# One transfer queue, straight casts and 168 transfers: a rewritten order for a clustered attention with a gated convolution behind it

## The chip, the cores and the metric

The kernel runs on one core of a Trainium2 chip. The metric is the device time of one execution in microseconds (us), lower is better; it is the span from the first to the last instruction plus about 2 us around it. PE is TensorE, DVE is VectorE, ACT is ScalarE, POOL is GpSimd, and SP is the sync engine, which here does nothing but issue DMA transfers.

## The reference

Four batches of eight heads, 768 tokens, 64 dimensions a head. Each token attends only to the tokens of its own cluster, where a cluster is the nearest of 16 centroids of that head. The attention's output (512 columns for a token) runs through a gated FFN with a convolution of three taps along the tokens.

```python
q_assign = argmax(einsum('bhsd,hcd->bhsc', q_n, c_n))   # and k_assign; q_n, k_n, c_n normalized
mask = q_assign[:, :, :, None] == k_assign[:, :, None, :]
scores = where(mask, q @ k^T / sqrt(64), -1e9)
x = softmax(scores) @ v                                  # heads side by side: (4, 768, 512)
h = maximum(x @ w_in, 0)                                 # 512 -> 1024
conv = sum of conv_w[k] * (h shifted by k - 1 along the tokens)
out = (h * sigmoid(conv)) @ w_out                        # 1024 -> 512
```

Inputs and outputs are float32 in HBM; q, k and v are 6.3 MB each.

## The kernel before, in words

The work goes by pairs of heads: `g` = 0 to 15, four pairs to a batch. Pair `g` is loaded, brought into a layout with the 64 dimensions on the partitions, assigned to clusters, and then used by two units `t`, one for each half of the queries: `t = 8 * batch + 4 * half + pair`, 0 to 31.

There is no loop that orders the work. A string `PLAN` lists some 1,660 steps, and each engine executes its own steps in the order of the string. SP is one such engine: a transfer waits there for its data and for its buffer, and all later ones on SP wait behind it. Steps that matter here, with the line of the profile:

- `LQ.g.part`, `LK.g.part` (L248, L255) load q and k on SP; `lq`, `lk` do the same from ScalarE's queue. `LV`/`lv` (L262, L264) load v. The string `KIND` gives each pair a way to be transposed. A pair of kind T is loaded by head (two parts, 128 partitions of 64-element rows) and transposed by PE: `T.g.c` (L275, four transposes into one PSUM bank), `Qd`/`Qa` copy it to `qkT`. A pair of kind B is loaded in four parts of 32 partitions (rows of 32 elements) and transposed in 32 x 32 blocks by VectorE: `D.g.o` (L283).
- `A.g` (L303) multiplies `qkT` with the centroids, `M0.g` to `M6.g` (L327 to L366) find the argmax on VectorE and write a code of the cluster into `pack`, `K.g` (L371) transposes `pack` on PE, `Bd`/`Ba` copy it to `spk`, and `BX.g` (L381, L383; `BA` from ScalarE's queue) transfers it into three rows of `ext`, the bias rows, which make the mask part of the score matmul.
- The 64 rows of `ext` above them are q and k in float16, for each head at partitions 0 to 63. `CQp.g.o` casts a whole `qkT` (128 partitions, both heads) into `c`, and `CX.g.h` (L294) transfers 64 partitions of `c` into `ext`. A few casts go straight: `CDa.g.h.o` casts head `h`'s 64 partitions of `qkT` into `ext`. The letter behind (p, a, d) names the engine: POOL, ScalarE, VectorE.
- `S.t.i` (L398) makes the scores, two matmuls for 256 keys; `E.t.i` (L410) takes the exponential on ScalarE; `V.t.u` (L429) multiplies with v and a column of ones; `NR`, `N` (L440, L445) normalize on VectorE into `x`.
- `XD.t` (L467) turns `x` by a DMA transpose into `xT`; `X.t` (L460) does it by three PE transposes, with `Ya`/`Yd` copying the result.
- `I` (L483) is x @ w_in, `Ra`/`Rd` (L496, L498) the relu into `hpad`, `c`, `a`, `b` and `cw`, `aw`, `bw` (L515, L517) the convolution, `H`/`Hw` the tanh, `G`/`Gw` (L554) the gate, `O` (L566) the product with w_out, `Fa`/`Fd` (L579, L581) its evacuation, `FX.b.tq` (L584) the store of 128 tokens.
- `_wl`/`_wlq` load a piece of the weights on SP or ScalarE's queue, `_wp`/`_wd` cast it, `_tp` builds matrices of taps on POOL, `_k` issues filler matmuls early on.

`qkT`, `c` and the v staging have two buffers each, `qk_in` four, `ext` and `v16` five.

Of the kernel before, what the change touches and what calls it, by code (L numbers as in the profile page):

```python
# [8 lines left out]
F32 = mybir.dt.float32  # L9
# [5 lines left out]
KIND = "TTTTTTTBBBBBBBBB"  # L15
# [129 lines left out]
def kernel(  # L145
# [11 lines left out]
    nc = tc.nc  # L157
# [425 lines left out]
    def store(b, tq):  # L583
        nc.sync.dma_start(out[b, P * tq : P * (tq + 1), :], o_t.pop((b, tq))[:])  # L584
# [246 lines left out]
```

## Time and profile before

| | |
|---|---|
| median of 3 runs | 268.18 us (267.23 to 268.81) |
| the profiled execution | 267.05 us, its span 265.1 us |
| mean granted clock of PE | 0.966 |
| busy: PE, DVE, ACT, POOL | 235.7, 212.5, 209.2, 63.6 us |
| transfers issued | 226: 190 by SP, 36 by ScalarE |
| DMA bytes | 38.75 MB |
| DMA queue of SP / of ScalarE | 30.68 MB, 56.9% / 7.69 MB, 16.2% of the span of 16 engines |

Busy times are unions of an engine's instructions. Matmuls are pipelined and short gaps between them count as busy, so PE's 89% is an upper figure. The granted clock tells in slices how fast PE was allowed to run. The chain that ended last is a path back through the execution: at each step what released an instruction.

### The profile page before, as it was taken

Reading aid. Unit: us, or ns where it says so; the run is one execution under the profiler, and the core shown is the slowest. Engines: PE = TensorE matmul, PEld = TensorE weight load, DVE = VectorE, ACT = ScalarE, POOL = GpSimd, SP = SyncE. Lnnn points to the kernel's source line nnn. Section 1 sums busy time; section 2 is a strip of 40 time slices with the busy share of each in tenths; the row PEclk is TensorE's granted clock in tenths of the full one; section 3 lists DMA queues with packets and bytes.
Section 4 is the critical chain, followed back from the end, with each engine's and each line's share of the span. In section 5 each row is a group of like instructions: output and inputs, shape, how many; then the busy total and the mean of one; then the engine's idle time right before and its main releaser. Section 6 shows DMA issues by size and latency. Waiting matters only on the chain.

```text
span 265.1 us, 6230 instructions
## 1 busy us (share of the span) xinstructions
PE 235.7 (89%) x2385; PEld 146.0 (55%) x2385; DVE 212.5 (80%) x414; ACT 209.2 (79%) x325; POOL 63.6 (24%) x107
## 2 busy tenths in 40 slices
PE   7878699979699985899989989996979999999994
PEld 7565376657365642566445545663345666565541
DVE  5777735875649996999999789995783999999971
ACT  5636758979498997699989889997567999995841
POOL 7313400463334353430450334000320000000000
PEclk9999979999799999799999999999797999999999
DMA  8986979999989697598979982775693220011244
GB/s 164 244 195 189 234 184 212 315 209 161 154 220 191 90 191 87 108 146 144 158 184 164 185 165 55 181 110 90 127 251 117 67 72 2 1 38 45 79 150 167
DMA packets 114825, 38.75 MB, mean 146 GB/s; under 512 B 106473, under 2 KB 108265, under 8 KB 114796
## 3 DMA queue, kind: packets, MB, share of 16 engines
q1 hardware_dynamic: 89470, 30.68, 56.9%
q10 hardware_dynamic: 25326, 7.69, 16.2%
q8 instruction: 18, 0.29, 0.5%
q14 instruction: 11, 0.09, 0.1%
HBM read 23.11 MB, written 6.29 MB: 111 GB/s over the span
## 4 chain that ended last, share of the span: by engine, by line
PE 40%; DMA 25%; DVE 18%; ACT 6%; issue 4%; SPq 4%; ACTq 1%; POOL 0%; DVEq 0%; POOLq 0%
PE sc L398 12%; PE flex L566 8%; DMA ext<-spk 7%; PE flex L483 6%; DVE cnv L517 6%; PE flex L429 6%; DMA qk_in<-in_q_dram 6%; DMA qk_in<-in_k_dram 5%; DMA ext<-c 4%; ACT attn L410 4%; DVE qkT L283 3%; SPq L248 3%; DMA xT<-x 2%; DVE hg L554 2%; PE flex L275 2%
## 5 line engine op out<-in xcount | busy, mean ns | idle before, releaser
L410 ACT ACTIVATE attn<-sc 128x768 f16<-128x768 f32 x192 | 146.7, 818 | 23.2 <-PE sc L398 22.3
L398 PE MATMUL sc<-ext 128*128 128x384 f16 x384 | 93.7, 336 | 13.5 <-DMA ext<-spk 6.7
L517 DVE SCALAR_TENSOR_TENSOR cnv<-hpad,cwcol,cnv 128x768 f16<-128x768 f16 (+2 forms) x72 | 63.8, 903 | 0.2
L429 PEld LDWEIGHTS <-attn 128*128 128x128 f16 x1152 | 51.4, 100 | 16.1 <-issue 3.2
L398 PEld LDWEIGHTS <-ext 128*128 128x128 f16 x384 | 33.5, 100 | 43.8 <-issue 20.6
L429 PE MATMUL flex<-v,attn 128*128 128x65 f16 x1152 | 54.9, 196 | 1.0 <-DVE x L445 1.0
L566 PE MATMUL flex<-w_out,hg 128*128 128x512 f16 x176 | 48.7, 390 | 0.0
L235 POOL CAST c<-qkT 128x768 f16<-128x768 f32 x26 | 25.2, 980 | 95.6 <-DVE qkT L283 28.3
L483 PE MATMUL flex<-xT,w_in 128*128 128x384 f16 x228 | 46.0, 329 | 1.8 <-DMA xT<-x 1.5
L483 PEld LDWEIGHTS <-w_in 128*128 128x128 f16 x256 | 23.9, 98 | 17.9 <-issue 3.4
L554 DVE SCALAR_TENSOR_TENSOR hg<-th,hpad 128x768 f16<-128x768 f32 (+3 forms) x34 | 31.4, 935 | 0.0
L545 ACT ACTIVATE th<-cnv 128x768 f32<-128x768 f16 (+2 forms) x30 | 25.6, 852 | 5.4 <-DVE cnv L517 5.3
L566 PEld LDWEIGHTS <-hg 128*128 128x128 f16 x192 | 18.1, 99 | 15.6 <-issue 0.9
L496 ACT ACTIVATE hpad<-flex 128x384 f16<-128x384 f32 x45 | 22.1, 517 | 1.4 <-PE flex L483 1.2
L283 DVE STREAM_TRANSPOSE qkT<-qk_in 128x768 f32<-128x768 f32 x18 | 17.2, 965 | 6.8 <-DMA qk_in<-in_q_dram 6.8
L303 PE MATMUL flex<-qkT,cT 128*32 128x384 f32 x128 | 13.8, 503 | 4.6 <-DVE x L445 4.1
L445 DVE TENSOR_TENSOR x<-flex,rec 128x384 f16<-128x384 f32 x32 | 17.5, 546 | 0.3
L235 POOL CAST v<-v_in 128x768 f16<-128x768 f32 x13 | 12.3, 957 | 16.0 <-DMA v_in<-in_v_dram 15.9
L327 DVE STREAM_TRANSPOSE sim<-flex 128x384 f32<-128x384 f32 x16 | 9.2, 576 | 7.0 <-PE flex L303 7.0
L515 DVE TENSOR_SCALAR cnv<-hpad,cwcol 128x768 f16<-128x768 f16 (+2 forms) x36 | 13.7, 382 | 0.7 <-ACT hpad L496 0.5
L440 DVE RECIPROCAL rec<-flex 128x6 f32<-128x6 f32 x32 | 5.9, 183 | 10.0 <-PE flex L429 9.9
L579 ACT ACTIVATE o_sb<-flex 128x512 f32<-128x512 f32 x17 | 10.0, 602 | 4.8 <-PE flex L566 4.8
(81 smaller groups left out, 193.2 us busy)
## 6 DMA issues: line engine op xcount, KB each, us to landing
out_dram<-o_sb SPq DMA_DIRECT2D x24, 256.0 KB, 3.2
ext<-c SPq DMA_DIRECT2D x30, 192.0 KB, 4.8
v_in<-in_v_dram SPq DMA_DIRECT2D x10, 384.0 KB
qk_in<-in_k_dram SPq DMA_DIRECT2D x28, 96.0 KB, 3.3
qk_in<-in_q_dram SPq DMA_DIRECT2D x27, 96.0 KB, 3.8
qk_in<-in_q_dram SPq DMA_DIRECT2D x12, 192.0 KB, 4.5
v_in<-in_v_dram ACTq DMA_DIRECT2D x6, 384.0 KB
qk_in<-in_k_dram SPq DMA_DIRECT2D x11, 192.0 KB, 4.6
```

What stands on the lines that cost most here:

```text
L235: (nc.vector if name == "d" else nc.gpsimd).tensor_copy(out=to, in_=src)
L283: nc.vector.transpose(qkT_of(g)[:, o, :], qk_t[g][:, o, :])
L398: nc.tensor.matmul(s[:, n, 0:HS], lhsT=ext_b[g % NE][:, h, 1, P * (kt + n) : P * (kt + n + 1)], rhs=ext_b[g % NE][:, h, 0, HS * a : HS * ( ...
L410: nc.scalar.activation(attn[t, i // 3][:, kt : kt + 2, :], sc[(6 * t + i) % 2][:, :, 0:HS], AF.Exp, scale=0.125)
L429: nc.tensor.matmul(avp(at)[:, u, 0 : D + 1], lhsT=attn[t, h][:, kt, P * jq : P * (jq + 1)], rhs=v16_b[g % NE][:, h, kt, 0 : D + 1], start= ...
L445: nc.vector.tensor_tensor(out=x16[t].rearrange("p jq (h d) -> p h jq d", h=2), in0=av[:, :, 0:D].rearrange("p (h jq) d -> p h jq d", h=2), ...
L483: nc.tensor.matmul(bank[at][:, 0:HS], lhsT=w_in16[:, r, 2 * u + f, :], rhs=xT[:, b % 2, r, HS * a : HS * (a + 1)], start=(r == 0), stop=(r ...
L496: nc.scalar.activation(to, src, AF.Relu)
L517: nc.vector.scalar_tensor_tensor(out=cnv, in0=src, scalar=w, in1=cnv, op0=ALU.mult, op1=ALU.add)
L545: nc.scalar.activation(th, cnv_t[key].rearrange("p (f s) -> p f s", s=N), AF.Tanh, scale=0.5)
L554: nc.vector.scalar_tensor_tensor(out=hg_b[b][:, 2 * u + fs.start : 2 * u + fs.stop, lo : lo + N], in0=th, scalar=1.0, in1=hpad(b, u)[:, fs ...
L566: nc.tensor.matmul(bank[at][:, 0:Dm], lhsT=hg_b[b][:, fb, P * tq : P * (tq + 1)], rhs=w_out16[:, fb, :], start=(fb == 0), stop=(fb == NFB ...
```

## The change

1. `KIND` has eight pairs of kind T (0 to 7) instead of seven; pairs 8 to 15 are of kind B.
2. k of a pair of kind T can be loaded whole by one transfer, both heads with 128 partitions outermost (`LK.g` without a part). Pairs 1 to 7 use it; pair 0's k comes in two parts from ScalarE's queue.
3. All casts of q and k go straight into `ext`, four for a pair over 64 partitions each: 51 on POOL (`CDp`), 7 on VectorE (`CDd`), 6 on ScalarE (`CDa`). No `CX` transfers and no `c` tile are left.
4. Batches 0 to 2 store two blocks of 128 tokens by one transfer (`FX.b.i`, i = 0 to 2), out of an `o_sb` of two blocks; batch 3 stores each block by itself.
5. The eight units of batch 0 turn `x` on PE (`X` with 4 `Ya` and 4 `Yd`) instead of by DMA; 20 `XD` remain, and 12 units use PE in all, for 28 and 4.
6. ScalarE's queue carries three transfers (the centroids and pair 0's k); everything else is on SP: 165.
7. The order of the whole `PLAN` is new, with small shifts of steps between engines (relus on VectorE 17 for 12, copies of `qkT` 15 and 9 for 13 and 8, output evacuations on VectorE 4 for 6).

Steps of each kind in the two orders:

| step | before | after | | step | before | after |
|---|---|---|---|---|---|---|
| LQ + lq | 50 | 48 | | CQ (p, a, d) | 30 | 0 |
| LK + lk | 50 | 41 | | CD (p, a, d) | 4 | 64 |
| LV + lv | 16 | 16 | | T | 21 | 24 |
| CX | 30 | 0 | | D | 18 | 16 |
| BX + BA | 18 | 18 | | X | 4 | 12 |
| XD | 28 | 20 | | Rd / Ra | 12 / 52 | 17 / 47 |
| FX | 24 | 15 | | Fd / Fa | 6 / 18 | 4 / 20 |
| _wl + _wlq | 8 | 8 | | V, S, E, I, O, K, A | the same | the same |

The diff, with the order cut to the stretches that the text speaks of:

```diff
-KIND = "TTTTTTTBBBBBBBBB"
+KIND = "TTTTTTTTBBBBBBBB"
...
+    "_par _k.32@4 T.0.0@0 _pk.0 _hz.2 lk.0.1 lk.0.0 _n0 _n1 _zd.0.0 _nq _n2 _n5 Qd.0.0 _k.16@4 T.0.1@1 Qd.0.1 "
+    "T.0.2@2 Qa.0.2 _pk.2 _hpk.0 _zp.0.1 _zp.1.1 CDp.0.0.0 LQ.1.0 LQ.1.1 LK.1 _n3@0 T.1.0@1 _n4 _k.2@4 A.0@2 "
...
+    "M6.0.0 _k.5@4 K.0.1@1 CDa.0.1.1 Ba.0.1 _k.12@4 T.2.0@1 T.2.2@2 T.2.1@0 Qa.2.2 BX.0.1 LK.3 K.0.0@3 Ba.0.0 "
+    "M3.1.0 M1.1.1 BX.0.0 LQ.3.0 LQ.3.1 M2.1.1 M4.1.0 M3.1.1 M5.1.0 M6.1.0 M4.1.1 _v.0 CVd.0 M5.1.1 Qa.2.0 "
...
-    "Qa.3.2 CQp.2.0 _zp.2.1 CVp.0 CQp.2.1 BX.1.0 T.3.0@1 LV.2 CX.2.1 CX.2.0 _cw0 S.1.0 E.1.0 LV.3 V.0.0@3 K.2@2 "
-    "S.1.1 V.0.1@3 V.0.2@3 S.1.2 Qd.3.0 Bd.2 Qd.3.1 CQp.3.1 _wp.2 _pk.0 A.3@0 M0.3 M1.3 M2.3 M3.3 M4.3 M5.3 "
+    "M6.2 Qd.3.0 K.2@0 Bd.2 Qd.3.1 S.0.5 V.0.0@1 V.0.1@1 S.1.0 A.3@2 BX.1.1 LV.2 _cw0 _wl.1 BX.2 LK.4 LQ.4.1 "
+    "LQ.4.0 LV.3 _wl.0 E.0.5 E.1.0 S.1.1 V.0.2@1 S.1.2 V.0.3@1 _cw1@0 E.1.1 S.1.3 E.1.2 S.1.4 V.0.4@1 M0.3 M1.3 "
...
+    "Gw.1.3.1 aw.1.3.0 BX.12 LK.14.1 LK.14.0 LV.14 LQ.14.0 LK.14.3 LQ.14.1 Ba.13 LQ.14.2 Ra.19.1 E.23.0 E.23.1 "
+    "LQ.14.3 BX.13 LQ.15.2 LK.14.2 LK.15.2 LK.15.1 LK.15.3 LQ.15.0 LK.15.0 LQ.15.3 LQ.15.1 S.23.2 E.23.2 "
...
+        elif part is None:
+            queue.dma_start(to[:, o, :], src[b, h0 : h0 + 2].rearrange("h (p j) d -> p j h d", p=P))
...
     def evac(name, b, tq):
-        o_t[b, tq] = rot.tile([P, Dm], F32, name="o_sb", tag="o_sb", bufs=BUFS["o_sb"])
-        src = bank[out_at[b, tq]][:, 0:Dm]
+        n = 1 if b == B - 1 else 2
+        if (b, tq // n) not in o_t:
+            o_t[b, tq // n] = rot.tile([P, 2, Dm], F32, name="o_sb", tag="o_sb", bufs=BUFS["o_sb"])
+        src, to = bank[out_at[b, tq]][:, 0:Dm], o_t[b, tq // n][:, tq % n, :]
...
+    def store(b, i):
+        if b == B - 1:
+            nc.sync.dma_start(out[b, P * i : P * (i + 1), :], o_t.pop((b, i))[:, 0])
+        else:
+            to = out[b, 2 * P * i : 2 * P * (i + 1), :].rearrange("(x p) d -> p x d", x=2)
+            nc.sync.dma_start(to, o_t.pop((b, i))[:])
```

More of the change, by code (lines that the diff above doesn't have):

```diff
@@ L575, in evac @@
     def evac(name, b, tq):
-        o_t[b, tq] = rot.tile([P, Dm], F32, name="o_sb", tag="o_sb", bufs=BUFS["o_sb"])
-        src = bank[out_at[b, tq]][:, 0:Dm]
+        n = 1 if b == B - 1 else 2
+        if (b, tq // n) not in o_t:
+            o_t[b, tq // n] = rot.tile([P, 2, Dm], F32, name="o_sb", tag="o_sb", bufs=BUFS["o_sb"])
+        src, to = bank[out_at[b, tq]][:, 0:Dm], o_t[b, tq // n][:, tq % n, :]
         if name == "a":
-            nc.scalar.activation(o_t[b, tq][:], src, AF.Copy, scale=0.5)
+            nc.scalar.activation(to, src, AF.Copy, scale=0.5)
         else:
-            nc.vector.tensor_scalar(out=o_t[b, tq][:], in0=src, scalar1=0.5, scalar2=None, op0=ALU.mult)
-    def store(b, tq):
-        nc.sync.dma_start(out[b, P * tq : P * (tq + 1), :], o_t.pop((b, tq))[:])
+            nc.vector.tensor_scalar(out=to, in0=src, scalar1=0.5, scalar2=None, op0=ALU.mult)
+    def store(b, i):
[4 more added lines that the diff above has]
+            nc.sync.dma_start(to, o_t.pop((b, i))[:])
     w_t = {}
```

227 rows, old and new, of the table PLAN are left out of this document.

## The prediction

> **What bounds the kernel now.** I read the page's busy times and slices first, then the same by stage, then the chain that ended last, then the waits.
>
> ```profile
> span 265.1 us, 6230 instructions
> PE 235.7 (89%) x2385; PEld 146.0 (55%) x2385; DVE 212.5 (80%) x414; ACT 209.2 (79%) x325; POOL 63.6 (24%) x107
> PEclk9999979999799999799999999999797999999999
> ```
>
> No engine is full over the span, and the granted clock dips in five of forty slices only. The stages below begin at the first scores, at the first scores of batch 1 (S.8.0) and of batch 3 (S.24.0); columns are elapsed time, busy time of each engine, granted clock, DMA share and GB/s.
>
> ```profile
> 0.00:21.85 21.85, 16.49 (x184) 13.31 (x184) 15.56 (x46) 10.13 (x17) 10.22 (x38) 1.00 0.99 201
> 21.85:70.22 48.37, 41.14 (x478) 27.97 (x478) 30.99 (x71) 37.74 (x54) 13.81 (x30) 0.96 1.08 210
> 70.22:178.20 107.98, 99.03 (x1048) 59.84 (x1049) 96.20 (x174) 95.72 (x148) 35.35 (x36) 0.97 0.84 149
> 178.20:265.10 86.90, 79.09 (x677) 44.88 (x675) 69.76 (x126) 65.65 (x108) 4.23 (x5) 0.96 0.35 93
> ```
>
> Batch 0 (the second row) has the DMA engines full (1.08) while VectorE has 17.4 us free. In the third row PE, VectorE and ScalarE are all near nine tenths, VectorE with 11.8 us free, so little can be won there. The clock's mean of 0.96 to 0.97 in the last three rows is 48.37 x 0.04 + 107.98 x 0.03 + 86.90 x 0.04 = 8.6 us at no speed, or 1.7 us for each of the five dips. The chain and the waits say what lies ahead of the dips:
>
> ```profile
> PE 40%; DMA 25%; DVE 18%; ACT 6%; issue 4%; SPq 4%; ACTq 1%; POOL 0%; DVEq 0%; POOLq 0%
> 17.64 4.07 DMA ext<-spk
> 27.77 5.94 DMA ext<-spk
> 64.28 5.90 DMA ext<-c
> 97.45 5.74 DMA qk_in<-in_q_dram
> 179.85 3.80 DMA qk_in<-in_q_dram
> 193.84 4.53 DMA ext<-spk
> ...
> PE sc L398 <- DMA ext<-spk: 6.7, 4, 2.6
> PE sc L398 <- DMA ext<-c: 3.1, 3, 2.3
> PE flex L483 <- DMA xT<-x: 1.5, 1, 1.5
> DVE qkT L283 <- DMA qk_in<-in_q_dram: 6.8, 4, 2.7
> ```
>
> A quarter of the chain is transfers, and each dip of the clock follows one: the bias rows of pair 2 at 27.77, the shift of cast q and k (CX) at 64.28, the q of pair 9 at 97.45, the q of pairs 14 and 15 at 179.85, the bias rows of pair 14 at 193.84. The kernel is bound by late transfers between stretches in which PE or VectorE is full.
>
> **The change part by part.** *The shifts go.* All 30 CX transfers leave, and the casts write the matmul operand directly.
>
> ```profile
> ext<-c SPq DMA_DIRECT2D x30, 192.0 KB, 4.8
> xT<-x SPq DMA_TRANSPOSE x28, 2.7
> DMA packets 114825, 38.75 MB, mean 146 GB/s; under 512 B 106473, under 2 KB 108265, under 8 KB 114796
> 13.56 1.20 SPq L294 DMA_DIRECT2D ext<-c  x2
> 51.12 3.25 SPq L467 DMA_TRANSPOSE xT<-x  x2
> SPq L248 <- DMA qk_in<-in_k_dram: 7.2, 4, 3.1
> SPq L467 <- DVE qkT L283: 6.0, 3, 2.4
> ```
>
> They are 30 x 0.196 MB = 5.9 of 38.75 MB, 15%, and 30 x 0.6 = 18 us of SP's issuing; from cast to operand each cost 4.8 us. Eight of the 28 DMA transposes go too (batch 0's), with 8 x 1.2 to 1.6 us of issuing. So the wait of 2.3 for CX and that of 1.5 for xT cannot come back as transfers: -3.8 us in batch 0. What is late next there is the bias rows (BX): each still takes 4 to 6 us from issue to use. Ahead of BX.2 on the queue are now a v and a weight load in place of two v loads and two shifts, and in the order 16 PE steps instead of 10 stand between K.2 and S.2.0, so I take half of its 2.6 us wait: -1.3. Of that stage's clock loss (1.9 us) half: -0.9.
>
> What pays for it:
>
> ```profile
> L460 PE MATMUL flex<-id,x 128*128 128x128 f16 x12 | 1.3, 219 | 0.0
> L233 ACT ACTIVATE xT<-flex 128x384 f16<-128x384 f16 x4 | 2.0, 495 | 1.5 <-PE flex L460 1.5
> L235 POOL CAST c<-qkT x26: 818/827/1595, 12.7 to 191.1; 128x768 f16<-128x768 f32 x26
> L235 POOL CAST ext<-qkT x1: 816/816/816, 9.5 to 9.5; 64x768 f16<-64x768 f32 x1
> L235 POOL CAST v<-v_in 128x768 f16<-128x768 f32 x13 | 12.3, 957 | 16.0 <-DMA v_in<-in_v_dram 15.9
> L706 POOL TENSOR_SCALAR taps<-id,cwcol 128x128 f16<-128x128 f16 x12 | 10.3, 860 | 0.0
> L235 POOL CAST w_out<-w_sb 128x512 f16<-128x512 f32 x8 | 5.7, 714 | 5.4 <-DMA w_sb<-in_moe_w_out_dram 5.4
> L235 DVE CAST c<-qkT 128x768 f16<-128x768 f32 x2 | 1.3, 628 | 0.0
> L235 DVE COPY qkT<-flex 128x512 f32<-128x512 f32 x13 | 8.9, 688 | 6.1 <-PE flex L275 5.9
> L283 DVE STREAM_TRANSPOSE qkT<-qk_in 128x768 f32<-128x768 f32 x18 | 17.2, 965 | 6.8 <-DMA qk_in<-in_q_dram 6.8
> L498 DVE TENSOR_SCALAR hpad<-flex 128x384 f16<-128x384 f32 x12 | 6.4, 543 | 0.8 <-PE flex L483 0.7
> L275 PE MATMUL flex<-id,qk_in 128*128 128x128 f32 x84 | 11.6, 276 | 1.9 <-DMA qk_in<-in_k_dram 1.6 <-DVE qkT L235 0.2
> ```
>
> PE gets 8 x 3 transposes of x, 24 x 0.11 = 2.6 us, 2.0 of it (six of the eight) in batch 0, and 12 f32 transposes for pair 7, 12 x 0.14 = 1.7 us, after S.8.0. PE has no room there, so both count in full. Their copies are 4 on ScalarE (2.0 us) and 4 on VectorE; VectorE's have no row and lie between 0.3 us (half of its cast of 768 columns) and 0.54 (the relu, from PSUM too and of the same shape); I take 0.5, nearer to the row that reads PSUM.
>
> A cast costs 816 ns over 64 partitions and 827 over 128, so POOL pays by the instruction: 51 x 0.816 - 27 x 0.82 = +19.5 us, against 201 us that POOL is idle. It matters only between S.4.0 and S.8.0, where the order gives POOL 8 casts of qk, 2 of v, 10 of taps and 10 of weights: 8 x 0.82 + 2 x 0.96 + 10 x 0.86 + 10 x 0.71 = 24 us, in a stretch that is half of batch 0's 48.4. Its cover is the time until batch 1; if that is gone, S.8.0 waits for the last cast.
>
> VectorE gets 7 direct casts (4.4), 4 xT copies (2.0), 5 relus (2.7), 2 qkT copies (1.4), and loses 2 block transposes (1.9), 2 casts (1.3) and 2 evacuations (by the qkT copy of that shape, 1.4): +5.9 us. Six casts, two xT copies and one qkT copy (3.8 + 1.0 + 0.7) are in batch 0, in 17.4 us of free time. Between S.8.0 and S.24.0 I count +4 relus, +2 xT copies, +2 qkT copies, +1 cast, one gate and one pair's argmax more (1.0 + 3.1, moved from elsewhere), less 2 transposes, 2 evacuations and smaller ones: about +5 us into 11.8 us free.
>
> *One queue.* ScalarE issued 36 transfers, now 3; SP 190, now 165. SP gains issue time, but everything waits in one order: a load stands behind XD (which waits for VectorE, up to 2.4 us), BX and FX. By the Trainium skill (DMA: Bandwidth & Descriptors, "Issuing engines are not separate DMA queues") transfers of all issuers share the same 16 engines, so one queue costs no bandwidth and splitting saves issue time only. No run here shows it yet; what this trace shows is SP held 7.2 us until earlier loads had landed.
>
> *Loads, stores.* One k load each for seven pairs saves 7 issues, 15 stores for 24 save 9; both are counted in SP's 165. Stores wait for a second evacuation, but the chain has none of batches 0 to 2, and in batch 3 each block is still stored alone. Zero.
>
> *The start.* BX.0.0 goes out behind the load LK.3 and Ba.0.0 stands behind a copy of pair 2's transposes, where ScalarE's own queue took 4.07 us at 17.64. Bounds: -1 (LQ.2 no longer behind a v load) to +4 (both halves of pair 0's bias rows as slow as those at 27.77, 2 x (5.94 - 4.07) = 3.7). I take +1.0, nearer to the end at which little stands ahead, since only one load does.
>
> *The middle.* Of the 6.8 us in which VectorE waits for q the longest, 2.7, is that of pairs 14 and 15, so at most 4.1 lie here. I take half of that and 1.0 of the clock's 3.2 as gained, -3.0, against 1.7 us of PE and 1.3 of VectorE's five that its free time does not take in: 0. Bounds -4 (all waits and no cost) to +5 (no gain).
>
> *The end.* After S.24.0 the work is the same to half a us. SP has 22 transfers there for 33, and pair 15's loads stand 11 us of PE work ahead of their transposes instead of 3, so the 2.7 us wait and one of two dips (1.7) should shrink; BX.14 and BX.15 are as tight as before (about 3 us of PE work after K). I take -2.0, bounds -4 to +2.
>
> Sum: start +1.0; batch 0 -3.8 - 1.3 - 0.9 + 2.0 = -4.0; middle 0; end -2.0: **-5.0 us**. The profiled execution took 267.05 us, 1.95 outside its span, and lies 0.4% under the median of 268.18; 267.05 - 5.0 = **262.0 us**.
>
> **Rivals.** *All stalls go*: every wait of PE for a transfer (6.7 + 3.1 + 1.5 = 11.3 us) and three of the five dips (5.1). For it: 15% fewer bytes where DMA is full. Against it: BX is untouched. -11.3 - 5.1 + 4.3 of new PE work gives 255.
>
> *Nothing moves*: five of the six late transfers shown are loads and bias rows, which stay; the 3.8 us that CX and xT give back are eaten by 4.3 us of PE transposes. 267 to 269.
>
> *Slower: one queue holds the loads back.* Behind a waiting XD or BX, the eight loads of a pair go out late, D waits, and PE cools. Each pair so delayed costs 2.7 + 1.7 = 4.4 us by the worst row above. For it: 67 loads of batches 1 to 3 now stand on SP between 20 XDs, and SP's queue is strict. Against it: SP has fewer transfers in each stage. With one pair more than now the forecast turns to 266.5, with three it is 275; it decides from two on, 271.
>
> *Slower or equal through POOL.*
>
> ```profile
> 11.80 0.35 DVE L336 TENSOR_TENSOR eqq<-sim,mx 128x192 f16<-128x192 f32 x1
> 12.71 0.82 POOL L235 CAST c<-qkT 128x768 f16<-128x768 f32 x1 [1.44 <-ACT qkT L233]
> 12.81 0.93 DVE L336 TENSOR_TENSOR eqq<-sim,mx 128x192 f16<-128x192 f32 x1
> ```
>
> The same VectorE operation took 0.35 us alone and 0.93 when a POOL cast had begun just before: it ended 0.21 us after the cast. With 24 more casts, each holding one such operation 0.6 us, VectorE loses up to 14 us; nearer the mean (half meet one, mostly in batch 0's free time), 3 us reach the end: 265. The Trainium skill (SBUF — State Buffer, "Who interferes with whom") says that a VectorE instruction with two SBUF inputs contends with a GpSimd instruction that reads SBUF, and whoever comes second is fully blocked; the rows agree.
>
> **How the numbers follow.** Forecast (258 to 266, the POOL loss at its top): 0.50. All stalls go: 0.12. Nothing moves: 0.14. One queue: 0.24. Half a percent (266.8 to 269.5) is about what a measurement here can tell: faster 0.62, same 0.14, slower 0.24. The range takes in the bounds: 255 (start -1, batch 0 -5, end -4) to 272 (two pairs late): about a tenth is left out on either side.
>
> **What would show it.** Right: DMA share in batch 0 near 0.85, no PE wait of over 1 us between S.4.0 and S.8.0, S.8.0 at 66 to 68 us, first scores at 22 to 24, PE busy up by some 4 us, POOL at 80 to 85. Wrong: SP waiting for VectorE ahead of loads with VectorE's transposes waiting for qk_in for over 7 us in all; six or more dips of the clock; S.8.0 waiting for a POOL cast.

## The result, and the profile after

| | before | after |
|---|---|---|
| median | 267.71 us (264.34 to 268.81, 4 runs) | 254.51 us (253.75 to 255.27, 4 runs) |
| ratio | | 0.9547 (95% interval 0.9449 to 0.9645) |
| forecast | | 262.0 us, range 255 to 272 |
| the profiled execution | 267.05 us | 254.97 us |

The changed kernel gained more than twice what was forecast (the profiled executions differ by 12.1 us, for 5.0), and lies half a us under the range. Before's own runs spread from 260.6 to 269.7 us over all comparisons below; the ratios leave out runs over 1.5% above the kernel's fastest, and the profiled executions of before and of "moving alone" below are among such longer ones, so a part of the differences by stage may be theirs. The version called "k by head and stores by single blocks" below takes as long as the changed kernel (254.46 us) and has the ratio 0.9667 (0.9562 to 0.9772) in another comparison: the gain is known to lie between about 9 and 12 us, and no better.

The changed kernel's page, busy times and the granted clock in 40 slices:

```profile
span 253.2 us, 6226 instructions
PE 232.9 (92%) x2419; PEld 148.0 (58%) x2419; DVE 224.8 (89%) x429; ACT 211.9 (84%) x328; POOL 82.0 (32%) x128
PEclk9998999999999988999999999999999999999999
```

Two dips are left of five, one of them ahead of the first scores. The same by stage, cut as in the prediction at S.0.0, S.8.0 and S.24.0 (elapsed; busy time of PE, PEld, VectorE, ScalarE, POOL; clock; DMA share; GB/s):

```profile
0.00:24.52 24.52, 18.84 (x192) 15.87 (x193) 16.74 (x48) 10.06 (x17) 10.23 (x39) 0.93 0.69 137
24.52:65.01 40.49, 39.73 (x497) 27.93 (x495) 33.22 (x78) 38.18 (x56) 20.20 (x36) 1.00 0.88 247
65.01:172.22 107.21, 98.25 (x1057) 59.98 (x1054) 104.56 (x178) 97.44 (x151) 43.10 (x45) 0.98 0.66 113
172.22:253.20 80.98, 76.07 (x683) 44.18 (x681) 70.24 (x128) 66.23 (x107) 8.47 (x9) 1.00 0.29 82
```

| stage | before | after | change | forecast |
|---|---|---|---|---|
| start, to S.0.0 | 21.85 | 24.52 | +2.7 | +1.0 |
| batch 0, to S.8.0 | 48.37 | 40.49 | -7.9 | -4.0 |
| middle, to S.24.0 | 107.98 | 107.21 | -0.8 | 0 |
| end | 86.90 | 80.98 | -5.9 | -2.0 |

In batch 0, PE now works 39.73 of 40.49 us: next to nothing makes it wait. In the middle VectorE works 104.56 of 107.21. The chain and the waits (total us, times, longest) say the same:

```profile
PE 41%; DVE 35%; ACT 9%; DMA 6%; issue 5%; SPq 2%; DVEq 0%; ACTq 0%
PE flex L374 <- DVE hpack L369: 3.4, 1, 3.4
PE sc L401 <- ACT attn L413: 2.1, 8, 0.5
PE flex L432 <- DVE x L448: 1.8, 1, 1.8
DVE qkT L286 <- DMA qk_in<-in_k_dram: 0.7, 1, 0.7
SPq L835 <- DMA out_dram<-o_sb: 1.4, 2, 0.9
```

Transfers have 6% of the chain, where they had 25%, and VectorE 35% for 18%. No score matmul waits for a transfer any more; VectorE waits 0.7 us for q and k, where it waited 6.8; and SP, which was held 7.2 us at loads until earlier loads had landed, waits for no other transfer but the last stores.

### The profile page after: what moved, and what is told of

The parts are those of the page before. It is cut to its first block, busy times and chain, and to the rows that moved or that the text cites. A ratio compares the mean times of both kernels' runs of the same rounds, so it can differ in the third digit from the quotient of the medians.

```text
span 253.2 us, 6226 instructions
## 1 busy us (share of the span) xinstructions
PE 232.9 (92%) x2419; PEld 148.0 (58%) x2419; DVE 224.8 (89%) x429; ACT 211.9 (84%) x328; POOL 82.0 (32%) x128
## 4 chain that ended last, share of the span: by engine, by line
PE 41%; DVE 35%; ACT 9%; DMA 6%; issue 5%; SPq 2%; DVEq 0%; ACTq 0%
PE sc L401 11%; DVE cnv L520 8%; PE flex L569 8%; ACT attn L413 6%; PE flex L432 6%; PE flex L486 5%; DVE qkT L286 4%; DVE hg L557 4%; PE flex L278 3%; DMA qk_in<-in_k_dram 3%; PE flex L306 3%; DVE cnv L518 2%; DMA qk_in<-in_q_dram 2%; DVE eqq L339 2%; DVE sim L330 2%
## 5 line engine op out<-in xcount | busy, mean ns | idle before, releaser
L413 ACT ACTIVATE attn<-sc 128x768 f16<-128x768 f32 x192 | 147.5, 822 | 12.1 <-PE sc L401 11.0
L401 PE MATMUL sc<-ext 128*128 128x384 f16 x384 | 92.0, 328 | 3.2 <-ACT attn L413 2.1
L236 POOL CAST ext<-qkT 64x768 f16<-64x768 f32 x51 | 49.2, 976 | 67.1 <-DVE qkT L286 40.6
L520 DVE SCALAR_TENSOR_TENSOR cnv<-hpad,cwcol,cnv 128x768 f16<-128x768 f16 (+2 forms) x72 | 65.3, 919 | 0.3
L432 PEld LDWEIGHTS <-attn 128*128 128x128 f16 x1152 | 50.3, 98 | 19.7 <-issue 6.4
L401 PEld LDWEIGHTS <-ext 128*128 128x128 f16 x384 | 32.0, 98 | 28.3 <-issue 13.7
L499 ACT ACTIVATE hpad<-flex 128x384 f16<-128x384 f32 x41 | 20.6, 516 | 0.7 <-PE flex L486 0.5
L278 PE MATMUL flex<-id,qk_in 128*128 128x128 f32 x96 | 15.5, 298 | 0.6 <-DVE qkT L236 0.2
L286 DVE STREAM_TRANSPOSE qkT<-qk_in 128x768 f32<-128x768 f32 x16 | 15.3, 960 | 0.7 <-DMA qk_in<-in_k_dram 0.7
L518 DVE TENSOR_SCALAR cnv<-hpad,cwcol 128x768 f16<-128x768 f16 (+2 forms) x36 | 15.0, 419 | 0.1
L278 PEld LDWEIGHTS flex<-id,qk_in 128*128 128x128 f32 x96 | 12.2, 155 | 2.4 <-issue 0.9
```

The lines of the kernel that those rows point to most:

```text
L236: (nc.vector if name == "d" else nc.gpsimd).tensor_copy(out=to, in_=src)
L278: nc.tensor.transpose(bank[at][:, P * i : P * (i + 1)], qk_t[g][:, o, P * j : P * (j + 1)], id128[:])
L286: nc.vector.transpose(qkT_of(g)[:, o, :], qk_t[g][:, o, :])
L401: nc.tensor.matmul(s[:, n, 0:HS], lhsT=ext_b[g % NE][:, h, 1, P * (kt + n) : P * (kt + n + 1)], rhs=ext_b[g % NE][:, h, 0, HS * a : HS * ( ...
L413: nc.scalar.activation(attn[t, i // 3][:, kt : kt + 2, :], sc[(6 * t + i) % 2][:, :, 0:HS], AF.Exp, scale=0.125)
L432: nc.tensor.matmul(avp(at)[:, u, 0 : D + 1], lhsT=attn[t, h][:, kt, P * jq : P * (jq + 1)], rhs=v16_b[g % NE][:, h, kt, 0 : D + 1], start= ...
```

## The experiments

Three theories for the gain: *relief* (the shifts and batch 0's DMA transposes are gone), *one queue*, and *the new order*. A fourth, *beside POOL* (VectorE's instructions are stretched while POOL casts), for why the middle stood still. All times are medians; the changed kernel is 254.5 us. Before was timed again beside each group of versions, with medians from 264.1 to 266.2 us; a ratio is to that before, and versions of different groups are safely told apart only by more than some 3 us.

### Parts of the change, done to the kernel before

**Straight casts alone.**

```diff
-CQp.2.0 ... CX.2.1 CX.2.0
+CDp.2.0.0 CDp.2.1.0 ...          (all pairs; no CX)
```

> The kernel before with one part of the change alone: every CQ becomes two straight casts on the same engine at the same place, and the 30 CX transfers are gone; queues, order, loads and stores stay. 'Relief': most of batch 0's gain is here, so faster than before by 3 to 7 us (261 to 265), batch 0 (start of S.0.0 to start of S.8.0) down from 48.8 to 43 to 45 us. 'Order': within 1.5 us of before or slower, since loads and bias transfers stay where they were. 'Beside POOL': the casts on POOL double, VectorE's busy time rises by 3 to 6 us from 212.5, and the middle loses 1 to 3 us of what batch 0 gains.

259.45 us, 0.9752 of before (0.9697 to 0.9806). Batch 0 and the middle, and the waits for transfers that are left:

```profile
22.61:66.47 43.86, 39.96 (x482) 26.95 (x480) 32.81 (x71) 36.72 (x52) 22.85 (x39) 1.00 0.95 204
66.47:171.41 104.94, 97.08 (x1054) 58.42 (x1051) 101.80 (x180) 96.57 (x149) 51.50 (x51) 1.00 0.72 122
PE sc L399 <- DMA ext<-spk: 1.6, 3, 0.8
DVE qkT L284 <- DMA qk_in<-in_q_dram: 3.6, 2, 2.6
```

As "relief" expected: batch 0 is 4.5 us shorter, and the bias rows' wait (ext<-spk) fell from 6.7 to 1.6 us although nothing was done to them: they had been late because of the shifts around them. "Beside POOL" had expected VectorE's busy time to rise by 3 to 6 us and the middle to lose 1 to 3. It rose by 8.4 (212.5 to 220.9), but the middle is 3.0 us shorter.

**Batch 0's X on PE as well.** `XD.0` to `XD.7` become `X` with 4 `Ya` and 4 `Yd`.

> The kernel before with two parts of the change: straight casts in place of all CQ and CX (alone it gave -6.7 us), and batch 0's 8 units turned by PE (X, Y) a few PE steps behind the places of XD. 'Relief' (transfers that wait and queue are what is lost, whoever they are): 2 to 4 us more, 255.5 to 257.5. 'Order' (the rest comes only with the new order): the PE transposes cost about what they save, 259 to 260.5.

256.95 us, 0.9734 (0.966 to 0.9807): 2.5 us less by the medians, though the ratios' intervals overlap almost wholly. In the one profile of each, S.8.0 comes at the same time (66.4 and 66.5 us; batch 0 takes 45.2 for 43.9 because S.0.0 comes 1.4 us earlier), and what is gained lies in the end (82.4 for 84.8 us), where no X was changed. "Relief" had the size; that X on PE brought it is not shown.

**And one queue as well.** `lq`, `lk`, `lv`, `_wlq`, `BA` become `LQ`, `LK`, `LV`, `_wl`, `BX` at the same places, all but pair 0's k.

> The same, and besides every load and bias transfer that ScalarE issued (all but pair 0's k) on SP's queue at the same place of the order. If one queue is a gain by itself: 1 to 3 us faster than the kernel with the two parts. If one queue only works in an order made for it (loads queue behind bias transfers and transposes that wait): 2 to 8 us slower than that kernel; what then lies between it and the changed kernel is the order's.

255.06 us (254.36 to 255.36), 0.9655 (0.9588 to 0.9723). This is the changed kernel's time without its order, without whole k loads, paired stores or the eighth pair of kind T. So the new order, with all that goes with it, is worth 0.5 us or nothing by the medians; by the ratios 1.1%, with overlapping intervals, and by the 0.9667 of the version with k by head nothing at all.

```profile
22.34:66.10 43.76, 40.90 (x499) 28.16 (x497) 34.04 (x72) 37.61 (x55) 22.36 (x39) 1.00 0.76 206
66.10:172.79 106.69, 97.41 (x1061) 58.84 (x1058) 103.11 (x181) 96.80 (x150) 49.70 (x51) 1.00 0.65 119
```

The changed kernel is 3.3 us shorter in batch 0, and pays 2.2 at the start, 0.5 in the middle and 0.4 in the end.

**One queue alone.**

> The kernel before with one part of the change alone: the 33 loads and bias transfers of ScalarE (all but pair 0's k) go on SP's queue at the same places; shifts and DMA transposes stay. If one queue is a gain by itself: 1 to 3 us faster than before, as behind the two other parts. If it only pays once the shifts and batch 0's DMA transposes are off that queue: 3 to 10 us slower than before, because loads then stand behind 30 shifts that wait for casts.

256.47 us, 0.9739 (0.9642 to 0.9835): by the ratio 6.9 us, far more than the 1 to 3 expected and as much as the straight casts alone, with all 30 shifts and 28 DMA transposes still there. Batch 0, the end, and the waits:

```profile
21.98:70.78 48.80, 42.51 (x478) 28.77 (x478) 29.64 (x70) 37.88 (x54) 14.28 (x30) 0.93 1.01 216
175.89:255.60 79.71, 75.76 (x677) 43.83 (x675) 70.00 (x126) 65.29 (x108) 4.24 (x5) 1.00 0.37 98
PE sc L397 <- DMA ext<-spk: 6.1, 5, 2.3
PE sc L397 <- DMA ext<-c: 3.6, 3, 1.8
DVE qkT L282 <- DMA qk_in<-in_k_dram: 0.9, 1, 0.9
DVE qkT L282 <- DMA qk_in<-in_q_dram: 0.5, 1, 0.5
SPq L254 <- DMA v_in<-in_v_dram: 0.5, 1, 0.5
```

It takes away other waits than the straight casts do. Batch 0 is as long as before, its shifts and bias rows as late; but VectorE's wait for q and k is down from 6.8 to 1.4 us, SP's loads no longer stand waiting for other loads to land (0.5 us in all, where one row of before had 7.2), and the clock's two dips in the end are gone, which is 7.2 us shorter. The two parts do not seem to add up: by the ratios they bring 2.5% and 2.6% alone and 3.4% together with X.

**The same, with ScalarE's time given back.** At each of the 33 places a ScalarE copy that nobody reads (two small constants share the convolution's buffers, to make room).

> The kernel before with one queue alone (256.47 us), and at each of the 33 places where ScalarE issued a transfer a ScalarE copy of 128x256 f16 that nobody reads (about 0.4 us, as an issue took). If the gain of one queue is ScalarE's time: back to 261 to 265. If it is the order in which loads arrive: 256 to 258.5.

252.06 us (250.73 to 254.64), 0.9501 (0.9382 to 0.962): not slower but 4.4 us *faster*.

```profile
L639 ACT ACTIVATE junk<-warm 128x256 f16<-128x256 f16 x33 | 14.0, 425 | 0.1
PE sc L400 <- DMA ext<-c: 2.6, 2, 2.1
PE sc L400 <- DMA ext<-spk: 2.3, 2, 1.5
```

14.0 us more of ScalarE's time did not take the gain back, so ScalarE's time alone does not explain it. What is left is when the loads are issued: with two queues SP's loads wait for transfers of either to land, with one they do not. Taking only that wait away was not tried, so this is the reading of the rows. Why the copies help was not settled; the rows show only that the score matmuls wait 4.9 us for transfers in place of 9.7. It also tells how much small shifts in time can do: between two orders, 4 us are not evidence without a trace.

### Parts undone in the changed kernel

**Shifts back for pairs 1 to 7**, 14 CX on SP.

> The changed kernel with one part undone in batch 0's pairs: pairs 1 to 7 are cast whole into c (CQ, on the engine of the first straight cast) and shifted into ext by 14 CX transfers on SP; order and queue stay as in the change. Theory 'relief' (batch 0's 8.5 us came from transfers that are gone, CX foremost): slower by 3 to 6 us, so 257.5 to 260.5, with waits for DMA back in front of the score matmuls of units 4 to 8. Rival 'order' (it came from loads and bias transfers that stand earlier in the one queue): within 1.5 us of the changed kernel. Theory 'beside POOL' (VectorE's instructions are stretched while POOL casts): seven pairs with two casts for four would take 1 to 2 us off VectorE and off the start, so even 253.

275.27 us, slower than before (1.0322, 1.0256 to 1.0388); +20.8 us, far above what any theory expected. **Batch 0's X by DMA again** (`XD.0` to `XD.7`):

> The changed kernel with batch 0's 8 units turned by DMA again (XD for X and Y), at the places of X. 'Relief': +1 to +3 us, 255.5 to 257.5, since PE is given back about 2 us of transposes and VectorE and ScalarE 4 copies each, while the x @ w_in of batch 0 waits again for transfers that queue among loads. Rival 'only moved': PE, VectorE and ScalarE have room there by the DMA version's 8 fewer triples, so -1 to 0.

263.71 us, +9.2, three times the most that "relief" expected; batch 0 is 5.0 us longer and the middle 5.1. **28 loads on ScalarE's queue again:**

> The changed kernel with 28 loads (those that ScalarE issued before) issued from ScalarE's queue again, at the same places of the order. 'One queue' (a single queue in order of need is itself worth something, because ScalarE issues loads between exponentials and the queues hold each other up): slower by 2 to 5 us, 256.5 to 259.5, ScalarE's busy time the same but its idle time before the exponentials longer. 'Relief' and 'order': within 1 us of the changed kernel, because bytes and places are the same.

280.13 us, +25.6, where 2 to 5 were expected. (k of pair 3 is among the 28, which ScalarE did not issue before.) Batch 0 with shifts and what held SP and PE; then batch 0 with two queues, and what held ScalarE and PE:

```profile
23.85:74.72 50.87, 42.96 (x498) 29.09 (x495) 31.96 (x77) 37.84 (x54) 19.31 (x36) 0.93 0.82 224
SPq L295 <- DVE c L234: 17.4, 4, 5.8
PE flex L276 <- DMA qk_in<-in_q_dram: 5.0, 2, 4.2
```

```profile
26.81:78.53 51.72, 41.85 (x494) 29.06 (x495) 33.44 (x77) 37.95 (x55) 22.35 (x39) 0.93 0.66 186
ACT attn L412 <- POOL v L235: 8.2, 1, 8.2
PE sc L400 <- ACT attn L412: 10.2, 12, 7.1
SPq L248 <- DMA v_in<-in_v_dram: 5.4, 1, 5.4
```

With the shifts SP stands 17.4 us at CX, waiting for casts, and q comes late. With two queues an exponential stands 8.2 us behind POOL's cast of v, which it does not need (a v load that needs its buffer does, and stands ahead of it on ScalarE; that is inferred from the order), and SP again waits for transfers. In both, the transfer engines are less busy than in the changed kernel (0.82 and 0.66 for 0.88): the queue is held, not full.

A CX does two things, wait and move. **Waiting alone:** 14 transfers of 32 bytes at CX's places, each reading a cast's result:

```diff
+dma_start(jw[0:1, i, j, :], ext[i][0:1, h, j, 0:16])     # 14 times
```

> The changed kernel with 14 transfers of 32 bytes that nobody reads, at the places where the undoing of batch 0's straight casts had its CX: each waits on SP for a pair's casts (of q, of k), as a CX does, and moves nothing to speak of. Undoing cost 20.8 us against the profile's own forecast of 3 to 6. 'Waiting' (SP executes in order, a transfer that waits for a cast holds the loads behind it): 60% or more of that is here, +12 to +20 us, with PE's waits for qk_in back. 'Bytes' (the SBUF-to-SBUF packets load the engines): within 2 us of the changed kernel.

270.17 us, +15.7. **Moving alone:** 14 transfers of CX's size from a constant tile.

> The changed kernel with 14 transfers of CX's shape and size (64 partitions x 3072 bytes, SBUF to SBUF, 0.2 MB each) at the same places, from a tile that is never written again into one that nobody reads, so that none waits for a cast. 'Waiting': only 14 issues and 2.8 MB more, +1 to +4 us. 'Bytes': +12 us or more, with the engines' share in batch 0 up from 0.88 to above 0.95.

266.26 us (263.11 to 268.71), +10 to +12. Batch 0 with waiting alone, and what held SP and PE; then batch 0 with moving alone, and what held SP:

```profile
24.47:70.09 45.62, 41.37 (x497) 28.26 (x495) 33.22 (x78) 37.70 (x55) 21.04 (x36) 0.96 0.68 200
SPq L648 <- POOL ext L238: 14.1, 2, 7.0
PE flex L280 <- DMA qk_in<-in_q_dram: 5.0, 1, 5.0
```

```profile
24.16:72.42 48.26, 42.98 (x498) 28.77 (x496) 33.86 (x79) 38.57 (x55) 19.01 (x34) 0.93 0.93 242
SPq L647 <- DMA jdst<-jsrc: 7.2, 3, 4.8
```

"Waiting" is three quarters of the undoing by itself, with the engines at 0.68; but the expectation that 14 transfers that wait for no cast cost 1 to 4 us fell. They cost 10 to 12, close to the 12 that "bytes" expected, with the engines at 0.93. But 7.2 us of it are SP waiting for one of them to land, and that wait is this version's own: all 14 write into the two halves of one tile. So moving was not tried without any waiting, and how much bytes cost by themselves stays open.

Each part undone cost more than it brought when done. My reading is that in batch 0 of the changed kernel, where PE works 39.73 of 40.49 us, a late load has no slack to hide in, and the next stage loses 5 to 11 us more. The order was also not made for what was put back; how much a place matters is seen below, where 16 shifts cost 5.0 us behind the loads and nothing ahead of them.

**k by head and stores by single blocks again**, 16 transfers more:

> The changed kernel with k of pairs 1 to 7 loaded by head again (14 transfers for 7) and the stores of batches 0 to 2 by single blocks (18 for 9), 16 transfers more on the one queue. 'Order' and 'relief': the same bytes, 16 more issues on an engine that only issues; within 0.7 us. Rival 'fewer transfers': SP is behind in batch 0, each transfer costs it about 0.1 to 0.3 us there, so +1.5 to +4 us.

254.46 us: no difference, as "order" and "relief" expected. SP does take longer (in batch 0 two issues for a pair's k take 1.2 to 1.3 us, and one of the whole 0.6 to 0.7), but nothing waits for it.

### The middle, and POOL

**One POOL cast more behind each of pairs 8 to 15**, read by nobody:

> The changed kernel with work added that nobody reads: after each POOL cast of pairs 8 to 15 one more POOL cast of 64x768, some 30 of about 1 us. 'Beside POOL': VectorE's instructions beside them are stretched as they are by the real casts (9 us more than before for 32 us more of POOL's casts, about a quarter of POOL's time), so VectorE's busy time rises by 6 to 9 us from 224.8 and the time by 3 to 7 us, 257.5 to 261.5, all of it in the middle. Rival: POOL has room (82 of 253 us) and what it does is free: within 1 us.

264.90 us, +10.4, above the range. The middle, the added casts, and one small VectorE operation (busy, mean ns); then that operation in the changed kernel, and in the kernel before:

```profile
64.46:180.75 116.29, 100.59 (x1056) 60.34 (x1053) 113.64 (x179) 97.95 (x151) 70.11 (x68) 0.97 0.55 107
L647 POOL CAST junk<-cT 64x768 f16<-64x768 f32 x31 | 33.9, 1094 | 0.9
L366 DVE TENSOR_TENSOR pack<-pack 128x24 f16<-128x24 f16 x14 | 6.2, 441 | 0.2
```

```profile
L365 DVE TENSOR_TENSOR pack<-pack 128x24 f16<-128x24 f16 x14 | 4.8, 341 | 0.2
```

```profile
L362 DVE TENSOR_TENSOR pack<-pack 128x24 f16<-128x24 f16 x14 | 2.9, 207 | 0.2
```

The same 14 operations take 207, 341 and 441 ns as POOL's casts grow. VectorE's busy time rises by 9.1 us in the middle and from 224.8 to 236.0 over the span: 0.36 us for each of the 31 casts, and the kernel pays 10.4. No wait of PE or VectorE for POOL appears in the middle, which leaves VectorE's stretched work. (The change itself made POOL's casts of q and k 23 us longer, 26.0 to 49.2, and not 32 as the expectation has it.)

**Fewer POOL casts there:** pairs 8 to 15 cast whole and shifted.

> The changed kernel with the other half of the casts undone: pairs 8 to 15 are cast whole into c and shifted by 16 CX transfers on SP; to make room the stores go by single blocks. 'Relief': the middle's transfer engines are only about two thirds busy (0.66), so the shifts cost little: 0 to +1.5 us. 'Beside POOL' (POOL's casts cost VectorE 9 us more than before in stretched instructions, and VectorE sets the middle): faster by 2 to 4 us, 250.5 to 252.5, with VectorE's busy time down by 3 to 5 us from 224.8. Rival 'order and queue': the 16 shifts wait on SP for a cast with the loads behind them, so slower by 2 to 4 us.

259.53 us, +5.0: VectorE's busy time does fall, by 6.9 us to 217.9, but pair 12's CX stands on SP behind seventeen loads of later pairs, and PE waits for it, as "order and queue" expected:

```profile
PE sc L399 <- DMA ext<-c: 5.6, 1, 5.6
```

**The same with CX ahead of the loads**, and the start repaired (below):

> The changed kernel with the start of run 'start' (-1.4 us), pairs 8 to 15 cast whole on POOL (16 casts of 128 partitions for 31 of 64) and shifted by 16 CX transfers that stand directly ahead of the pair's bias transfer, and stores by single blocks. If POOL's casts eat the middle's gain and the shifts cost little where the engines have room: middle 3 to 6 us shorter, 247 to 251. If shifts on the one queue cost as much as in batch 0: 255 or more, with PE waiting for CX.

252.50 us, 0.9604 (0.9513 to 0.9695): above the 247 to 251 expected, and 7.0 us under the version before it. The start is worth 1.4 of that, and the place of the shifts about the rest. **Relus to ScalarE instead**, alone and with the start:

> The changed kernel with the nine relus of VectorE between S.8.0 and S.24.0 moved to ScalarE (9 x about 0.55 us off VectorE, 9 x about 0.5 us onto ScalarE, which is 97.8 of 107.5 us busy there). If VectorE's own work sets the middle: 2 to 4.5 us faster, 250 to 252.5. Rival: ScalarE is as close to the bound, the relus delay its exponentials: within 1 us or slower.

> The changed kernel with the start of run 'start' and the nine relus on ScalarE. If both add: 249 to 251.5. If the relus do nothing: 253.

254.86 and 252.61 us: the relus do nothing, as the rivals had it. **Both, and pairs 14 and 15 straight:**

> The changed kernel with the repaired start, pairs 8 to 13 cast whole and shifted (12 CX transfers ahead of the pair's bias transfer), pairs 14 and 15 straight, four relus of the middle on ScalarE, stores by single blocks. If VectorE's load, the casts beside it and the relus add up: 249 to 251.5. If the middle is held by three engines at once (PE 97, VectorE 101, ScalarE 98 of 107 us in best1), nothing more comes: 252 to 253.

252.30 us. The middle in best1 and in best2:

```profile
62.05:168.66 106.61, 96.72 (x1056) 59.58 (x1053) 101.11 (x179) 97.33 (x151) 30.81 (x32) 1.00 0.65 133
```

```profile
62.57:170.46 107.89, 97.50 (x1057) 59.46 (x1053) 100.26 (x170) 100.02 (x160) 42.81 (x44) 1.00 0.72 114
```

VectorE got 3.5 and 4.3 us less to do, and the middle is 0.6 us shorter and 0.7 longer. With both, in best3, it is 2.1 us shorter (105.1), and the end takes that back (83.6 for 81.0 us). Loading VectorE costs at once, relieving it brings little. PE, VectorE and ScalarE are all at nine tenths there, which would explain it; no version relieved all three, so that is not shown. That the POOL casts ate the middle's gain was my reading of the trace after; best1 does not bear it out, though its 16 shifts are a load that the changed kernel does not have.

### The start

**Pair 1's four casts on ScalarE, K.0.0 ahead of T.2.1:**

> The changed kernel with the start put otherwise: pair 1's four casts go from POOL to ScalarE, and K.0.0, Ba.0.0 and BX.0.0 come ahead of T.2.1, Qa.2.2 and LK.3. If the 2.95 us that the changed kernel loses ahead of S.0.0 come from the POOL casts of pairs 0 and 1 that stretch the argmax (val 0.83 us for 0.25) and from K.0.0 standing behind T.2: S.0.0 starts 2 to 4 us earlier than 25.3, and the end follows by 1 to 3: 251.5 to 253.5. Rival: the start is hidden behind the loads of the later pairs, so S.0.0 is earlier and S.8.0 is not: within 0.7 us of the changed kernel.

253.07 us (252.54 to 254.29), 1.4 less than the changed kernel, and than the version with k by head that was timed beside it (254.46). In the changed kernel and in this one (start us, us, what):

```profile
12.58 0.83 DVE L345 TENSOR_TENSOR val<-eqq,iota 128x192 f16<-128x192 f16 x1
14.30 0.79 DVE L353 TENSOR_SCALAR hpack<-best 128x12 f16<-128x12 f32 x1
17.65 0.22 PE L374 MATMUL flex<-id,hpack 128*128 128x128 f16 x1 [3.42 <-DVE hpack L369]
18.88 2.62 PE L278 MATMUL flex<-id,qk_in 128*128 128x128 f32 x12
21.34 0.22 PE L374 MATMUL flex<-id,hpack 128*128 128x128 f16 x1
```

```profile
13.20 0.26 DVE L344 TENSOR_TENSOR val<-eqq,iota 128x192 f16<-128x192 f16 x1
14.03 0.17 DVE L352 TENSOR_SCALAR hpack<-best 128x12 f16<-128x12 f32 x1
```

In the changed kernel POOL casts of pairs 0 and 1 run beside the argmax, the two operations shown take three to five times as long, and the second transposed code (21.34) waits behind pair 2. Both were changed at once, so how much each of them costs is not told apart. S.0.0 now starts at 22.2 us for 24.5, as expected, S.8.0 at 64.5 for 65.0: most of it is lost again in batch 0, and the median keeps 1.4 us, with intervals that touch. best1, best2 and best3, which carry it, lie at 252.3 to 252.6 us, 2 us under the changed kernel and 2.3 under the relus alone (254.86), timed beside the first two. They are the fastest versions of it that were run, with the kernel before with one queue and copies beside them; their ratios (0.954 to 0.962) do not lie under the changed kernel's 0.9547, since before was faster beside them, so the 2 us rest on the medians.

## Why the prediction was wrong in size

Two steps failed. One queue had no term in the sum, and is worth 6.9 us alone, most of it in the end; and half of the bias rows' wait and of the clock's loss was kept in batch 0, where both went. The size of the second is partly a matter of the cut: up to S.8.0 the change gained 5.2 us for 3.0 forecast, behind it 6.7 for 2.0.

**Batch 0 (-4.0 forecast, -7.9).** The forecast removed the waits for CX and xT, half of the bias rows' wait and half of the clock's loss, and charged 2.0 us of PE work. Measured by the stage's rows: PE's idle time went from 48.37 - 41.14 = 7.2 to 40.49 - 39.73 = 0.8 us, 6.4 less where 5.1 were forecast (2.3 + 1.5 + 1.3), and the clock from 0.96 to 1.00, the whole 1.9 us for half of it. The failed step is "what is late next there is the bias rows": they were late because of the shifts on their queue, as the straight casts alone showed (6.7 to 1.6 us over the span), while one queue alone, with the shifts still there, left it at 6.1. The straight casts alone shorten the stage by 4.5 us and bring S.8.0 from 70.2 to 66.5; with X as well it is 66.4, with X and one queue 66.1, in the changed kernel 65.0. The rest of the 7.9 us is thus mostly time that the new order moved ahead of S.0.0. PE's work at full clock is 41.14 x 0.96 = 39.5 before and 39.7 after, so the charge of 2.0 us did not show in the stage, although the work is there, 18 of these 36 transposes with 2.0 us in batch 0:

```profile
L463 PE MATMUL flex<-id,x 128*128 128x128 f16 x36 | 3.8, 219 | 0.0
```

The rows of PE's single lines in batch 0 add up to 52.1 us before and 55.2 after, for 41.1 and 39.7 us in which PE was busy: matmuls of different lines overlap in time, and more so after. That this took in the 2.0 us is likely, but not shown.

**The end (-2.0 forecast, -5.9).** The 2.7 us wait and one of two dips were to shrink, because pair 15's loads stand earlier. Both dips went: 86.90 x 0.04 = 3.5 us, and 2.9 us of PE's idle time (7.8 to 4.9). One queue alone does all of this with every load at its old place (79.7 us), so the place was not the cause. With one queue the end takes 79.4 to 81.0 us in every version that adds nothing there, with two it takes 82.4 to 86.9.

**One queue (priced at nothing in the sum).** Alone it is worth 6.9 us by its ratio. The prediction had the row that the runs point to, SP held 7.2 us until loads had landed, and used it only as a remark; that this wait is the cause was not tried by itself. The rule beside it, from the Trainium skill (DMA: Bandwidth & Descriptors, "Issuing engines are not separate DMA queues"), that another issuer saves issue time and adds no bandwidth, agrees with the runs as far as it goes: one queue lost nothing. What the rule does not say, and the runs show, is that a second issuer can cost: 6.9 us in before's order and 25.6 in the changed kernel's.

**The rivals.** "All stalls go" (255, chance 0.12) has the time to half a us, and the waits and three dips that it names are gone. Its "against" (BX is untouched) was the mistake. Its reason, fewer bytes, is at most a part of it: one queue moves the same bytes and clears the end. It also had no term for what the start lost (2.7 us) and for VectorE's new work in the middle, so its 255 is in part luck. "One queue holds the loads back" (chance 0.24) did not occur, though its mechanism is real: 14 small waits on the queue cost 15.7 us. Nor did it fail because few waits were left. XD had waited for VectorE for up to 5.4 us in before (not 2.4, as the prediction read), and in the changed kernel SP stands longer at the bias rows than before, where the longest was 4.1 us:

```profile
SPq L384 <- DVE rec L443: 14.9, 3, 6.4
SPq L384 <- DVE mx L333: 9.0, 1, 9.0
```

Yet the loads behind them come in time. By these rows it is not the number of waits that decides, but whether something needed soon stands behind one.

**The middle (0 forecast, -0.8).** Right in size. The waits for transfers went, and VectorE's busy time rose by 8.4 us (96.20 to 104.56) where I had counted 5. The stretching that I named as a rival is real: the small operations above took 207 ns before and 341 after. It agrees with the Trainium skill (SBUF — State Buffer, "Who interferes with whom"), by which a VectorE instruction with two SBUF inputs contends with a GpSimd instruction that reads SBUF. But with the middle's POOL casts halved the middle is only 0.6 us shorter. What holds the stage at 103 to 108 us in every fast version is probably three engines near nine tenths, which the prediction had said.

**The start (+1.0 forecast, +2.7).** Inside its bounds, but not by the bias rows' place on the queue: SP is done with LK.3 at 19.85 us and issues BX.0.0 at 21.89, as soon as its data is there. That data is late: POOL's casts stretch the argmax, and K.0.0 comes at 21.3, behind twelve transposes of pair 2.

**What would show it.** DMA share in batch 0 (0.88 for 0.85), no PE wait of a us between S.4.0 and S.8.0, POOL's 82.0 us: right, the last partly by luck, since a cast took 976 ns on average and not 816. S.8.0 came at 65.0, a us ahead of its window; first scores at 24.5, half a us behind; PE's busy time fell by 2.8 us instead of rising by 4. Most of that difference is the clock by an estimate from its means: its loss fell by 5.7 us (265.1 x 0.034 = 9.0 before, 253.2 x 0.013 = 3.3 after). None of the signs of being wrong came: all of them stood for a slower kernel.

## What to carry to other kernels

A transfer that waits, on a queue that is executed in order, holds back every later one, and that costs when one of them is needed soon. When one kind of waiting transfer is removed, expect the waits of its neighbours to go too, and the clock dips behind them, until an engine is full; forecast from that floor, not by halves. Ask what a second issuer makes the first one wait for before giving it no price. Parts that remove the same stalls need not add up, and here a part undone in the finished kernel cost far more than it had brought, so price a part in the kernel where it was put in. Where three engines share a stage at nine tenths, loading one of them costs at once, relieving one brings little.

## What the runs showed of the hardware

- VectorE paid 0.36 us for each added POOL cast of 1.09 us (224.8 to 236.0 us for 31), and operations of 24 columns were hit hardest (207 to 441 ns).
- VectorE copies 128x384 float16 from PSUM in less than the half us that I took:

```profile
L236 DVE COPY xT<-flex 128x384 f16<-128x384 f16 x4 | 1.3, 354 | 1.4 <-PE flex L463 1.4
```

- 33 ScalarE copies that nobody reads (14.0 us) made a kernel 4.4 us faster by the medians of two comparisons (ratio 0.9501 for 0.9739); the cause stays open.
